# Planner constants of an fp32 attention and Fourier kernel on one core: durations, engine occupancy and latency apart

## The chip, the cores and the metric

The kernel runs on one core of one Trainium2 chip. The metric is the device time of one execution in microseconds (us). Before the change the median of three runs is 2807.93 us (2806.95 to 2810.59).

## The reference

Two independent blocks, whose results stand side by side in the output (2048 x 2048 fp32). Block A is attention with 32 heads of 32 columns that share one key and one value (multi-query). Block B is a Fourier mixing layer, the real part of a two-dimensional transform, written as products with four constant matrices.

```
q = (x @ wq) as 32 heads of 32;  k = x @ wk;  v = x @ wv      # x 2048x1024
p = softmax(q k^T / sqrt(32));   A = concat_heads(p @ v) @ wo
a = xB @ hid_re^T;  b = xB @ hid_im^T                          # 2048x1024
B = seq_re @ a - seq_im @ b                                    # seq: 2048x2048
out = concat([A, B], axis=-1)
```

## The kernel before

**Products.** Every large product other than attention's output is made of fp32r pieces. An operand is split into a high part (a cast to fp32r, tile names ending in h) and a low part (the operand minus its high part, ending in l); a block of 128 x 512 is summed over high times high, low times high and high times low. One group of `rest` has 12 to 48 such matmuls into one PSUM bank (psb). Right operands are tiles r, rh, rl, left ones m, mh, ml. The Fourier block's two stages are each done with seven products of half size (`PRODUCTS`), so operands are often sums of two blocks, which GpSimd adds. Some of these sums are stored once and loaded again (as). The high part is cast by VectorE (by ScalarE at the start of the kernel), the low part is subtracted by GpSimd, or by VectorE when the planner finds GpSimd late. Results leave PSUM through tile h and are added up in DRAM through tile y.

**Attention.** A unit is one of 32 pairs of a block of 512 queries and a group of four heads; it has 32 steps. A step has two parts. A *row* (`row`) is two matmuls into pss, 128 queries against 1024 keys; VectorE takes the row maximum (nm), ScalarE the exponentials and their sum. Only the maximum and the sum are kept. A *column* (`col`) is two matmuls into pst, the scores transposed with the maximum already subtracted inside the product; ScalarE takes the exponential into p. When the columns of four key chunks (eight steps) are there, `pv` multiplies them with v: a **burst** of matmuls with 32-column weights into a psb bank, the four heads at four places of the array. An fp32 matmul of a burst stands once in the program and as two records in the trace. `pv(k)` issues a burst whole; `pv(k, 0)` and `pv(k, 1)` issue its halves with a column and rows between. There are 128 bursts. pss has two buffers, pst one, psb two banks that groups of products, bursts and a small transpose (ident) share. After each unit VectorE turns the sums into factors, and the transpose brings the maxima into rows for the next pass.

**What sets the order.** Nothing is ordered at run time. The program is written by a planner in the same file. `Plan` keeps, for ScalarE, VectorE, GpSimd and the DMA queue of SP, the time from which the engine is free; `Plan.task` takes the engines that may do a task, its duration, what it depends on and a priority, and `Plan.run` (called up to the time `T` at which TensorE stands) starts the most urgent task that is known. A task that is finished makes its successors known, after the latency `LAG` of the engine that takes them. TensorE's stream is written by the main loop: at time `T` it puts the next burst, column, row or product of `rest` (the "fill") whose dependencies the plan holds to be done; each matmul costs `MM`, a burst `PV_US`, and a result is ready `MM_END` after the last one. Where nothing is ready, `T` moves on. So a planned duration decides on which instruction stands where, for all engines, and the order is fixed before the kernel runs. `prepare` makes the tasks of an operand (load, sum, high, low), `open_unit` those of a unit. A burst is cut in two where `STEP` times the steps that remain exceeds the matmul time that remains by more than `SPARE` allows:

```
if n + 2 * NB < total and STEP * (total - n) > (BODY - fill) * MM + (total - n) * (4 * MM + PV_US[4] / 8) - SPARE:
    pv(k, 0)
```

All engine instructions go through one helper and stand at its line, L57, in the profile; they are told apart by tile names.

Of the kernel before, what the change touches and what calls it, by code (L numbers as in the profile page):

```python
# [9 lines left out]
F32 = mybir.dt.float32  # L10
F32R = mybir.dt.float32r
# [27 lines left out]
ORDER_1, TURNED, ORDER_2 = (4, 1, 2, 3, 0, 6, 5), (3, 4, 5), (1, 0, 4, 2, 3, 5, 6)  # L39


MM, MM_END, PV_US, T_US = 0.232, 0.17, {2: 1.95, 4: 3.65}, 0.3
NB = 4
EXTRA = 2
LAG = {"act": 0.1, "dve": 0.1, "pool": 0.15, "sp": 0.3, "pe": 0.1}
ISSUE, RATE, FLIGHT = 0.42, 300.0, 2.0

# [17 lines left out]
class Plan:  # L65
# [50 lines left out]
    def run(self, until):  # L116
        while True:
            best = self.next()
            if best is None or best[0] > until:
                return  # L120
            at, e = best
            r, t = min((x for x in self.known[e] if x[0] <= at), key=lambda x: (x[1].prio, x[1].seq))
            for f, _ in t.engines:
                self.known[f] = [x for x in self.known[f] if x[1] is not t]
            t.on = e
            t.emit(e) if len(t.engines) > 1 else t.emit()
            us = t.us[e] if isinstance(t.us, dict) else t.us
            end = self.free[e] = at + us
            if e == "sp":
                self.dma = max(self.dma, end) + t.kb / RATE  # L130
                end = self.dma + FLIGHT
            self.finish(t, at, end)
# [48 lines left out]
def tile_kernel(ctx: ExitStack, tc, xT, wq, wkv, wo, xbT, wT, cT, out):  # L181
    nc = tc.nc
    te = Ordered(tc, nc.tensor)
    act = Ordered(tc, nc.scalar)
    dve = Ordered(tc, nc.vector)
    gp = Ordered(tc, nc.gpsimd)
    sp = Ordered(tc, nc.sync)
    eng = {"act": act, "dve": dve, "pool": gp}
    scale = float(DH) ** -0.5
    plan = Plan()  # L190
# [46 lines left out]
    ohr = Ring(misc, "oh", 1, [P, W], F32R)  # L237
    ovr = Ring(misc, "ov", 1, [P, W], F32)
    rbr = Ring(misc, "rb", 1, [P, W], F32)
# [278 lines left out]
    def prepare(it):  # L518
        kind, at = it.kind, it.need
        early = at < START  # L520
        hs, ls = (it.split[0], None) if it.split else (hir[kind].take(), lor[kind].take())
        hs.users.append(it.used)
        src = [landed[k] for k in it.after]
        if it.pre:
            def fetch(a):
                t = (hir if a == 0 else lor)[kind].make((hs, ls)[a])
                d = it.pre()[a]
                t = t[:, :d.shape[1]]
                move(t, d)
                if a:  # L530
                    it.lo = t
                else:
                    it.hi = t
            h = plan.task("sp", ISSUE, lambda: fetch(0), deps=[*hs.deps, *src], prio=at - 30, kb=256, order=o_hi[kind])
            l = plan.task("sp", ISSUE, lambda: fetch(1), deps=[*hs.deps, *src], prio=at - 30, kb=256, order=[h])
            o_hi[kind] = [l]
            it.ready = [h, l]
            return
        loads, it.t, it.raw = [], [None] * len(it.srcs), []
        for a, (ap, _) in enumerate(it.srcs):  # L540
            slot = it.room[0] if it.room else raw[kind][a].take()
            it.raw.append(slot)

            def load(a=a, ap=ap, slot=slot):
                d = ap()
                if it.room:
                    t = slot.tile[:, it.room[1]].bitcast(F32)
                else:
                    t = raw[kind][a].make(slot)
                if kind == "m":  # L550
                    t = t[:, :d.shape[1], :d.shape[2]]
                it.t[a] = t
                sp.dma_start(t.rearrange("p (a b) -> p a b", a=d.shape[1]) if kind == "r" and len(d.shape) == 3 else t, d)
            deps = slot.deps if not it.room else [before[it].ready[1]] if it in before else []
            o_load[kind] = [plan.task("sp", ISSUE, load, deps=[*deps, *src], prio=at - 30, kb=256, order=o_load[kind])]
            loads += o_load[kind]
        got = loads
        if len(it.srcs) > 1:
            def comb():
                (gp.tensor_add if it.srcs[1][1] > 0 else gp.tensor_sub)(it.t[0], it.t[0], it.t[1])  # L560
            got = [plan.task("pool", 1.33, comb, deps=loads, prio=at)]
            it.raw[1].users += got

        def high(on):
            if it.split and kind == "r":
                t = hs.tile
                it.hi, it.lo = (t[:, 2 * it.split[1] + x].bitcast(F32R) for x in range(2))
            elif it.split:
                t = hs.tile[:, it.split[1]]
                it.hi, it.lo = (t[:, x * 8 * DH:(x + 1) * 8 * DH].rearrange("p (a b) -> p a b", a=4).bitcast(F32R)  # L570
                                for x in range(2))
            else:
                it.hi, it.lo = hir[kind].make(hs), lor[kind].make(ls)
            if kind == "m" and not it.split:
                _, n, w = it.t[0].shape
                it.hi, it.lo = it.hi[:, :n, :w], it.lo[:, :n, :w]
            act.activation(it.hi, it.t[0], AF.Copy) if on == "act" else dve.tensor_copy(it.hi, it.t[0])
        h = plan.task((("act", 0.0), ("dve", 0.3)) if early else (("dve", 0.0), ("act", 1e6)), 0.65, high,
                      deps=[*got, *hs.deps], prio=at, order=[] if it.split else o_hi[kind])
        if not it.split:  # L580
            o_hi[kind] = [h]
        l = plan.task((("dve", 0.0), ("pool", 1.0)) if early else (("pool", 0.0), ("dve", 0.8 if kind == "r" else 2.5)), {"dve": 0.75, "pool": 1.33},
                      lambda on: eng[on].tensor_sub(it.lo, it.t[0], it.hi.bitcast(F32)), deps=[h], prio=at)
        it.raw[0].users.append(l)
        it.ready = [h, l]
# [22 lines left out]
    first_p = -1e5  # L608

    def open_unit(u):  # L610
        b, g = units[u]
        U = Unit()
# [11 lines left out]
        for r in range(SU):  # L624
            s = u * SU + r
            i, j = divmod(r, 2)

            def top(r=r, s=s, i=i, j=j):
                if r == 0:
                    nmr.make(U.nm), lsr.make(U.ls)  # L630
                dve.tensor_reduce(U.nm.tile[:, j, i:i + 1], rowps[s], axis=AX.X, op=ALU.max, negate=True)
            mx = plan.task("dve", 1.23, top, deps=[rowT[s], *(U.nm.deps if r == 0 else ())], prio=first_p + s - 44)
            plan.task("act", 1.14, lambda s=s, i=i, j=j: act.activation(
                rowps[s], rowps[s], AF.Exp, bias=U.nm.tile[:, j, i:i + 1], accum_out=U.ls.tile[:, j, i:i + 1]),
                deps=[mx], prio=first_p + s - 43.6, into=rexp[s],
                order=[cexp[s - SU - LEAD - EXTRA]] if s >= SU + LEAD + EXTRA else [])

# [48 lines left out]
        for c in range(NC):  # L686
            slot = pr.take()
            slot.users.append(pvH[u][c // 2])
            for hp in range(2):
                n = u * SU + 2 * c + hp  # L690

                def ex(n=n, hp=hp, slot=slot, c=c):
                    if hp == 0:
                        pt[u, c] = pr.make(slot)
                    act.activation(pt[u, c][:, 2 * hp:2 * hp + 2], colps[n], AF.Exp)
                plan.task("act", 1.05, ex, deps=[colT[n], *(slot.deps if hp == 0 else ())], prio=first_p + n, into=cexp[n])

        U.ov = ovr.take()
        U.add = []
# [5 lines left out]
                    dve.tensor_add(U.ov.tile, U.ov.tile, pvps[u, k])  # L705
            U.add.append(plan.task("dve", 0.7, ad, deps=[pvT[u][k], *(U.ov.deps if k == 0 else U.add[-1:])], prio=-1e3))
        U.oh = ohr.take()
        a = plan.task("dve", 0.76, lambda: dve.tensor_mul(U.ov.tile, U.ov.tile, U.rb.tile), deps=[U.add[-1], *U.inv], prio=-5)
        U.rb.users.append(a)
        h = plan.task("dve", 0.45, lambda: dve.tensor_copy(ohr.make(U.oh), U.ov.tile), deps=[a, *U.oh.deps], prio=-5)  # L710
        if u + 1 < NU:
            l = plan.task("dve", 0.75, lambda: dve.tensor_sub(U.ov.tile.bitcast(F32R), U.ov.tile, U.oh.tile.bitcast(F32)),
                          deps=[h], prio=-5)
            U.oh.users.append(l)
            U.oh.users.append(store(lambda: oh_d[b][g], lambda: U.oh.tile, [h], level(u * SU + 48), key=("oh", b, g), bits=True))
            U.ov.users.append(store(lambda: ol_d[b][g], lambda: U.ov.tile, [l], level(u * SU + 48), key=("ol", b, g), bits=True))
        else:
            s = rbr.take()
            l = plan.task("dve", 0.75, lambda: dve.tensor_sub(rbr.make(s, F32R), U.ov.tile, U.oh.tile.bitcast(F32)),
                          deps=[h, *s.deps], prio=-5)  # L720
            U.low = s
        U.end = [h, l]
# [127 lines left out]
        issue(o.us, emit, [o.done])  # L850
        bank_task[b] = o.freed

    SLACK, AHEAD, RUN, STEP, SPARE = 0.05, 30, 20, 2.55, 10.0

    def odd_ones():
        for o in odds:
# [51 lines left out]
    s = k = 0  # L908
# [146 lines left out]
```

## Time and profile before

| | |
|---|---|
| runs, median (lowest to highest) | 2807.93 us (2806.95 to 2810.59) |
| the profiled execution's own time | 2807.72 us |
| its span, first to last instruction | 2805.9 us |
| granted TensorE clock, mean | 0.998 |
| DMA | 518.64 MB, 185 GB/s over the span |
| TensorE: products, rows, columns, bursts | 5664, 2048, 2048, 4096 records |
| ScalarE: row and column exponentials | 1024 of 1086 ns, 1024 of 1027 ns |
| VectorE: row maxima | 1024 of 1221 ns |

The busy time of an engine is a union over the span; an instruction of ScalarE or VectorE may start before the record of the one ahead has ended, so durations add up to more than the engine's busy time. A matmul's record is longer than the distance to the next one, since they are pipelined; the time of TensorE's stream is read from start to start.

### The profile page before, as it was taken

To read this page: it belongs to the slowest core of one execution; us is meant where nothing else is said; L and a number is where in the kernel's file an instruction comes from. 1 tells how busy PE (TensorE), PEld (TensorE's weight loads), DVE (VectorE), ACT (ScalarE), POOL (GpSimd) and SP (SyncE) were. 2 spreads that over 40 slices of the span, in tenths; PEclk is the share of its full clock that TensorE was granted. 3 is DMA by queue.
4 is the path that set the end of the run, shared out by engine and by line. 5 is a ranking of instruction groups with operands and counts; after the bars stand their busy time and mean duration, and the time that the engine had idled before them with its cause. 6 is when DMAs were issued, how large, how long until landed. Compare 5 with 4: busy or idle time off the path is not lost.

```text
span 2805.9 us, 40813 instructions
## 1 busy us (share of the span) xinstructions
PE 2783.4 (99%) x13904; PEld 1929.3 (69%) x13904; DVE 1972.9 (70%) x2394; ACT 2225.0 (79%) x3204; POOL 1418.1 (51%) x1073
## 2 busy tenths in 40 slices
PE   8999999999999999999999999999999999999999
PEld 6876666666666666666676676776666776767667
DVE  6887767768878777778667668678777787676510
ACT  5688888888888888898888887888787888878741
POOL 2664425547666446535526537568768566540000
PEclk9999999999999999999999999999999999999999
DMA  9664546657776547635736726458749654453445
GB/s 291 189 195 136 168 142 201 216 188 248 234 239 204 163 148 244 210 110 165 253 95 203 231 89 200 148 173 263 248 156 290 189 168 153 132 154 114 143 147 158
DMA packets 336465, 518.64 MB, mean 185 GB/s; under 512 B 35712, under 2 KB 100736, under 8 KB 336256
## 3 DMA queue, kind: packets, MB, share of 16 engines
q1 hardware_dynamic: 336256, 516.04, 58.6%
q8 instruction: 109, 1.79, 0.3%
q14 instruction: 100, 0.82, 0.1%
HBM read 376.70 MB, written 138.15 MB: 183 GB/s over the span
## 4 chain that ended last, share of the span: by engine, by line
PE 93%; DVE 4%; DMA 1%; POOL 1%; issue 1%; ACT 0%; SPq 0%; POOLq 0%; DVEq 0%; ACTq 0%
PE psb L57 59%; PE pst L57 17%; PE pss L57 17%; DVE nm L57 1%; DVE rh L57 1%; DMA r<-as 1%; DVE h L57 0%; ACT pss L57 0%; POOL ml L57 0%; DVE mh L57 0%; POOL rl L57 0%; DVE md L57 0%; DMA a<-y 0%; DMA y<-a 0%; DVE l L57 0%
## 5 line engine op out<-in xcount | busy, mean ns | idle before, releaser
L57 DVE TENSOR_REDUCE nm<-pss 128x1 f32<-128x1024 f32 x1024 | 1238.4, 1221 | 427.6 <-PE pss L57 424.7
L57 ACT ACTIVATE p<-pst 128x1024 f32<-128x1024 f32 x1024 | 1051.4, 1027 | 350.6 <-PE pst L57 347.8
L57 ACT ACTIVATE pss<-pss,nm 128x1024 f32<-128x1024 f32 x1024 | 1111.6, 1086 | 131.1 <-DVE nm L57 129.0
L57 PE MATMUL psb<-rh,mh 128*128 128x512 f32 x1756 | 694.0, 395 | 2.1 <-DVE h L57 1.6
L57 PE MATMUL psb<-rh,ml 128*128 128x512 f32 x1756 | 690.7, 393 | 0.0
L57 PE MATMUL psb<-rl,mh 128*128 128x512 f32 x1756 | 690.6, 393 | 0.0
L57 PE MATMUL pst<-qst,kst 128*128 128x512 f32 x2048 | 663.1, 405 | 0.1
L57 POOL TENSOR_TENSOR ml<-m,mh 128x512 fp32r<-128x512 f32 x330 | 436.8, 1324 | 416.8 <-DVE mh L57 285.9
L57 PE MATMUL pss<-kst,qst 128*128 128x512 f32 x2048 | 624.9, 396 | 4.8 <-ACT pss L57 4.7
L57 PEld LDWEIGHTS pst<-qst,kst 128*128 128x128 f32 x2048 | 369.9, 188 | 230.3 <-issue 110.7
L57 PE MATMUL psb<-p,v 128*32 128x512 f32 x4096 | 478.4, 597 | 0.5 <-DVE h L57 0.5
L57 PEld LDWEIGHTS pss<-kst,qst 128*128 128x128 f32 x2048 | 382.2, 188 | 101.4 <-ACT pss L57 12.6
L57 POOL TENSOR_TENSOR m<-m,m 128x512 f32<-128x512 f32 x200 | 264.1, 1321 | 246.2 <-DMA m<-in_cT_dram 159.4
L57 PEld LDWEIGHTS psb<-rh,mh 128*128 128x128 f32 x1756 | 329.6, 188 | 82.5 <-DVE h L57 4.2
L57 PEld LDWEIGHTS psb<-rl,mh 128*128 128x128 f32 x1756 | 330.0, 188 | 77.4
L57 PEld LDWEIGHTS psb<-rh,ml 128*128 128x128 f32 x1756 | 329.6, 188 | 77.3
L57 POOL TENSOR_TENSOR y<-y,h 128x512 f32<-128x512 f32 x192 | 258.6, 1352 | 227.6 <-DVE h L57 200.3
L57 POOL TENSOR_TENSOR rl<-r,rh 128x512 fp32r<-128x512 f32 x190 | 253.3, 1339 | 228.0 <-DVE rh L57 214.5
L57 PEld LDWEIGHTS psb<-p,v 128*32 128x32 f32 x4096 | 113.8, 109 | 262.6 <-issue 253.3
L57 DVE CAST mh<-m 128x512 fp32r<-128x512 f32 x329 | 198.7, 606 | 13.8 <-PE psb L57 12.2
L57 ACT ACTIVATION_READ_ACCUMULATOR pss<-pss,nm 128x1 f32 x1024 | 207.5, 203 | 0.0
L57 POOL TENSOR_TENSOR r<-r,r 128x512 f32<-128x512 f32 x120 | 158.0, 1320 | 60.5 <-DMA r<-a 32.0
(77 smaller groups left out, 981.9 us busy)
## 6 DMA issues: line engine op xcount, KB each, us to landing
m<-in_cT_dram SPq DMA_DIRECT2D x384, 256.0 KB, 3.7
r<-a SPq DMA_DIRECT2D x192, 256.0 KB, 4.2
y<-a SPq DMA_DIRECT2D x128, 256.0 KB, 3.4
a<-y SPq DMA_DIRECT2D x128, 256.0 KB, 2.8
r<-in_wT_dram SPq DMA_DIRECT2D x96, 256.0 KB, 4.1
m<-in_xbT_dram SPq DMA_DIRECT2D x96, 256.0 KB, 3.3
y<-y SPq DMA_DIRECT2D x96, 256.0 KB, 3.9
as<-r SPq DMA_DIRECT2D x80, 256.0 KB, 4.4
```

The source lines that it names most:

```text
L57: return lambda *a, **k: self.tc.keep_in_program_order(f(*a, **k))
```

## The change

The planner's constants change, and two lines of its account. The time until an engine is free again is now less than a task's duration by `OVER` (0.1 us on ScalarE, 0.08 on VectorE, 0.06 on GpSimd), so that occupancy and latency are apart; durations of tasks are set anew; a matmul's result counts as ready 0.1 us after its time, not 0.17; `STEP` is 2.45, not 2.55. `T_US` was not used. Nothing else differs: the same tasks, tiles and buffers.

```diff
-MM, MM_END, PV_US, T_US = 0.232, 0.17, {2: 1.95, 4: 3.65}, 0.3
+MM, MM_END, PV_US = 0.232, 0.1, {2: 1.98, 4: 3.65}
+OVER = {"act": 0.1, "dve": 0.08, "pool": 0.06, "sp": 0.0}
...
-            end = self.free[e] = at + us
+            end = at + us
+            self.free[e] = max(end - OVER[e], at + us / 2)
...
-        h = plan.task((("act", 0.0), ("dve", 0.3)) if early else (("dve", 0.0), ("act", 1e6)), 0.65, high,
+        h = plan.task((("act", 0.0), ("dve", 0.3)) if early else (("dve", 0.0), ("act", 1e6)), 0.72 if kind == "r" else 0.62, high,
...
-            mx = plan.task("dve", 1.23, top, deps=[rowT[s], *(U.nm.deps if r == 0 else ())], prio=first_p + s - 44)
-            plan.task("act", 1.14, lambda s=s, i=i, j=j: act.activation(
+            mx = plan.task("dve", 1.22, top, deps=[rowT[s], *(U.nm.deps if r == 0 else ())], prio=first_p + s - 44)
+            plan.task("act", 1.22, lambda s=s, i=i, j=j: act.activation(
...
-                plan.task("act", 1.05, ex, deps=[colT[n], *(slot.deps if hp == 0 else ())], prio=first_p + n, into=cexp[n])
+                plan.task("act", 1.055, ex, deps=[colT[n], *(slot.deps if hp == 0 else ())], prio=first_p + n, into=cexp[n])
...
-    SLACK, AHEAD, RUN, STEP, SPARE = 0.05, 30, 20, 2.55, 10.0
+    SLACK, AHEAD, RUN, STEP, SPARE = 0.05, 30, 20, 2.45, 10.0
```

The other lines of the diff set durations of smaller tasks of VectorE and GpSimd: the low parts (0.75 to 0.8, 1.33 to 1.34), and the end of a unit (0.76 to 0.77, 0.45 to 0.6, 0.75 to 0.8).

What this does to the order is seen at three places of TensorE's stream. The first is a burst about a quarter into the program. In a row, pst is a column, pss a row, psb from rh or rl a product, psb from p and v a burst; a whole burst has 16 instructions. Before:

```order
L57 MATMUL psb<-p,v 32x512 x8
L57 MATMUL pst<-qst,kst 128x512 x2
L57 MATMUL pss<-kst,qst 128x512 x4
L57 MATMUL psb<-p,v 32x512 x8
L57 MATMUL pst<-qst,kst 128x512 x2
L57 MATMUL psb<-rh,mh 128x512
L57 MATMUL pss<-kst,qst 128x512 x2
```

The same stretch after the change, with the step ahead of the burst:

```order
L58 MATMUL pst<-qst,kst 128x512 x2
L58 MATMUL psb<-rl,mh 128x512
L58 MATMUL psb<-rh,ml 128x512
L58 MATMUL psb<-rh,mh 128x512
L58 MATMUL pss<-kst,qst 128x512 x2
L58 MATMUL psb<-rl,mh 128x512
L58 MATMUL psb<-rh,ml 128x512
L58 MATMUL pst<-qst,kst 128x512 x2
L58 MATMUL psb<-p,v 32x512 x16
L58 MATMUL pst<-qst,kst 128x512 x2
L58 MATMUL pss<-kst,qst 128x512 x4
```

The burst is whole, with one column and two rows behind it, and the step ahead of it, from one column to the next, has nine matmuls. In the whole program 188 bursts and halves became 135.

The second place is the transpose (ident) that ends a unit, before, where it falls between two groups of products: the product behind it is the first of a group, and uses the bank that the product ahead of it ended.

```order
L57 MATMUL psb<-rl,mh 128x512
L57 MATMUL psb<-rh,ml 128x512
L57 MATMUL psb<-ident,m_1_270 128x128
L57 MATMUL pss<-kst,qst 128x512 x2
L57 MATMUL psb<-rh,mh 128x512
```

After, the transpose of the same unit stands behind a whole burst and the rows that follow it:

```order
L58 MATMUL psb<-p,v 32x512 x16
L58 MATMUL pst<-qst,kst 128x512 x2
L58 MATMUL pss<-kst,qst 128x512 x4
L58 MATMUL psb<-ident,m_1_270 128x128
L58 MATMUL psb<-rh,mh 128x512
```

There the burst has taken its own bank, and the distance from a group's end to the next use of its bank has grown.

The third place is the end of the last unit, where the products of `rest` run out; the pss rows behind the last burst belong to the last eight groups. Before:

```order
L57 MATMUL pst<-qst,kst 128x512 x2
L57 MATMUL psb<-rh,ml 128x512
L57 MATMUL psb<-rh,mh 128x512
L57 MATMUL psb<-rl,mh 128x512
L57 MATMUL psb<-rh,ml 128x512
L57 MATMUL psb<-rh,mh 128x512
L57 MATMUL psb<-rl,mh 128x512
L57 MATMUL psb<-rh,ml 128x512
L57 MATMUL psb<-rh,mh 128x512
L57 MATMUL psb<-rl,mh 128x512
L57 MATMUL psb<-rh,ml 128x512
L57 MATMUL psb<-rh,mh 128x512
```

Two products (psb from rl and rh) and the last burst follow these rows. After:

```order
L58 MATMUL pst<-qst,kst 128x512 x2
L58 MATMUL psb<-rh,mh 128x512
L58 MATMUL psb<-rl,mh 128x512
L58 MATMUL psb<-rh,ml 128x512
L58 MATMUL pst<-qst,kst 128x512 x4
L58 MATMUL psb<-p,v 32x512 x16
L58 MATMUL pss<-rh,mh 128x512
```

The products ended earlier against the columns, and the last two columns and the last burst follow each other with none between.

More of the change, by code (lines that the diff above doesn't have):

```diff
@@ L581, in prepare @@
             o_hi[kind] = [h]
-        l = plan.task((("dve", 0.0), ("pool", 1.0)) if early else (("pool", 0.0), ("dve", 0.8 if kind == "r" else 2.5)), {"dve": 0.75, "pool": 1.33},
+        l = plan.task((("dve", 0.0), ("pool", 1.0)) if early else (("pool", 0.0), ("dve", 0.8 if kind == "r" else 2.5)), {"dve": 0.8, "pool": 1.34},
                       lambda on: eng[on].tensor_sub(it.lo, it.t[0], it.hi.bitcast(F32)), deps=[h], prio=at)
@@ L707, in open_unit @@
         U.oh = ohr.take()
-        a = plan.task("dve", 0.76, lambda: dve.tensor_mul(U.ov.tile, U.ov.tile, U.rb.tile), deps=[U.add[-1], *U.inv], prio=-5)
+        a = plan.task("dve", 0.77, lambda: dve.tensor_mul(U.ov.tile, U.ov.tile, U.rb.tile), deps=[U.add[-1], *U.inv], prio=-5)
         U.rb.users.append(a)
-        h = plan.task("dve", 0.45, lambda: dve.tensor_copy(ohr.make(U.oh), U.ov.tile), deps=[a, *U.oh.deps], prio=-5)
+        h = plan.task("dve", 0.6, lambda: dve.tensor_copy(ohr.make(U.oh), U.ov.tile), deps=[a, *U.oh.deps], prio=-5)
         if u + 1 < NU:
-            l = plan.task("dve", 0.75, lambda: dve.tensor_sub(U.ov.tile.bitcast(F32R), U.ov.tile, U.oh.tile.bitcast(F32)),
+            l = plan.task("dve", 0.8, lambda: dve.tensor_sub(U.ov.tile.bitcast(F32R), U.ov.tile, U.oh.tile.bitcast(F32)),
                           deps=[h], prio=-5)
@@ L718, in open_unit @@
             s = rbr.take()
-            l = plan.task("dve", 0.75, lambda: dve.tensor_sub(rbr.make(s, F32R), U.ov.tile, U.oh.tile.bitcast(F32)),
+            l = plan.task("dve", 0.8, lambda: dve.tensor_sub(rbr.make(s, F32R), U.ov.tile, U.oh.tile.bitcast(F32)),
                           deps=[h, *s.deps], prio=-5)
```

## The prediction

> **What bounds the kernel now.** I read the page's first and fourth parts first.
>
> ```profile
> span 2805.9 us, 40813 instructions
> PE 2783.4 (99%) x13904; PEld 1929.3 (69%) x13904; DVE 1972.9 (70%) x2394; ACT 2225.0 (79%) x3204; POOL 1418.1 (51%) x1073
> PE 93%; DVE 4%; DMA 1%; POOL 1%; issue 1%; ACT 0%; SPq 0%; POOLq 0%; DVEq 0%; ACTq 0%
> ```
>
> TensorE is busy nearly all the time and 93% of the chain that ends last, so the time is the length of TensorE's own stream plus the moments at which it waits. Nothing done elsewhere saves anything unless it shortens one of these two. The profiled execution took 2807.72 us, 1.8 more than its span, and 0.2 under the median of the three runs.
>
> Next, the timeline of TensorE at a burst of output matmuls (psb<-p,v; 16 records are a half, 32 a whole).
>
> ```profile
> 1301.97 1.09 PE L57 MATMUL pss<-kst,qst 128*128 128x512 f32 x4
> 1302.99 1.92 PE L57 MATMUL psb<-p,v 128*32 128x512 f32 x16
> 1304.85 0.73 PE L57 MATMUL pst<-qst,kst 128*128 128x512 f32 x2
> 1305.41 0.40 PE L57 MATMUL psb<-rh,mh 128*128 128x512 f32 x1
> ...
> 1317.93 0.63 PE L57 MATMUL pst<-qst,kst 128*128 128x512 f32 x2
> ...
> 1358.32 0.63 PE L57 MATMUL pst<-qst,kst 128*128 128x512 f32 x2
> 1358.88 3.64 PE L57 MATMUL psb<-p,v 128*32 128x512 f32 x32
> 1362.45 0.74 PE L57 MATMUL pst<-qst,kst 128*128 128x512 f32 x2
> 1363.03 1.10 PE L57 MATMUL pss<-kst,qst 128*128 128x512 f32 x4
> ```
>
> From 1305.41 to 1317.93 lie 54 matmuls without a burst: 12.52 / 54 = 0.232 us from start to start, one **step** below. A half burst: from 1301.97 to 1305.41 are 3.44 us with six other matmuls in them, 3.44 - 6 x 0.232 = 2.05. A whole burst: from 1358.32 to 1363.03 are 4.71 us with four others, 4.71 - 4 x 0.232 = 3.78. These prices hold the slower change into and out of a burst. Two halves cost 4.10, **0.32 us more than one whole**.
>
> Third, what TensorE waited for.
>
> ```profile
> PE psb L57 <- ACT p L57: 5.6, 1, 5.6
> PE pss L57 <- ACT pss L57: 4.7, 5, 1.9
> PE psb L57 <- DVE m L57: 3.8, 3, 3.2
> PE psb L57 <- DVE h L57: 2.1, 7, 0.5
> PE psb L57 <- POOL ml L57: 1.8, 1, 1.8
> ```
>
> The first and the last are the start of the kernel, before and at its first products (7.4 together). There remain about 10.6 us in the body: even a perfect order can take no more from waits than this and what follows them.
>
> **The change, part by part.**
>
> *Bursts.* By the order of TensorE's instructions, before has 68 whole bursts and 120 halves, after 121 whole and 14 halves: 53 pairs become whole. 53 x 0.32 = **-17.0 us**, all on TensorE's stream. Everything else that TensorE issues keeps its count. What the halves hid was ScalarE: the softmax's exponentials stand still during a burst. I cost that under the cadence below.
>
> *Banks.* At nine places in the order before, all while halves are used, a group of products starts too soon after the last use of its bank: a group ends, a transpose (ident) follows into the other bank, one pair of score matmuls, then the next group.
>
> ```profile
> 699.91 0.39 PE L57 MATMUL psb<-rh,ml 128*128 128x512 f32 x1
> 700.17 0.71 PE L57 MATMUL pss<-kst,qst 128*128 128x512 f32 x2
> 700.41 0.69 DVE L57 TENSOR_SCALAR h<-psb 128x512 f32<-128x512 f32 x1 [0.24 <-PE psb L57]
> 701.16 0.50 PE L57 MATMUL psb<-rh,mh 128*128 128x512 f32 x1 [0.28 <-DVE h L57]
> ```
>
> The bank is free 701.16 - 699.91 = 1.25 us after its last matmul; without the wait the next product would have started at 700.17 + 2 x 0.232 = 700.63, so 0.53 at most was lost here, 0.28 by the row's own idle time. Between the sum of the idle (2.1) and 9 x 0.53 = 4.8 I take 3.5. In the order after, the transpose stands inside a group, and one place with a distance under 1.25 us is left (4 steps, 0.9 us): **-3.2 us**.
>
> *The end.* Before, 13 products stand between the last pair of column scores (pst) and the last burst. After, the products run out: three of them, then two pairs of pst at once, then the burst. A pst pair can follow the last one only when its exponential is done.
>
> ```profile
> 1338.08 0.63 PE L57 MATMUL pst<-qst,kst 128*128 128x512 f32 x2
> 1338.75 1.02 ACT L57 ACTIVATE p<-pst 128x1024 f32<-128x1024 f32 x1 [0.20 <-PE pst L57]
> 1344.78 1.09 ACT L57 ACTIVATE pss<-pss,nm 128x1024 f32<-128x1024 f32 x1 [0.76 <-DVE nm L57]
> 1346.79 1.09 ACT L57 ACTIVATE pss<-pss,nm 128x1024 f32<-128x1024 f32 x1
> ```
>
> That is 0.67 from the start of the pair to its exponential, 1.02 for it, and 0.04 to release TensorE (the 0.04 is a row below): 1.74 us. The order gives 5 steps (1.16), then 2 (0.46), then 2 again before the burst: 0.58 + 1.28 + 1.28 = **+3.1 us**. There is no cover: no products are left. Each of these stops is under 1.3 us; that matters for the clock, next.
>
> *The planner's numbers.* ScalarE's and VectorE's instructions are now planned to follow each other sooner (about 0.1 us less occupancy), and the order follows. Before, successive pst pairs stand nine steps apart 461 times and ten 258 times, mostly in turn; now nine 703 times and ten 16 times. Nine steps are 2.09 us. ScalarE can do this: two successive row exponentials, with the column one between, start 1346.79 - 1344.78 = 2.01 apart when nothing holds them. So it is hidden, with 0.08 us to spare in each step. The chain through VectorE has this form (from the chain of waits):
>
> ```profile
> 2111.91 1.14 DVE nm L57
> ...
> 2113.14 1.21 ACT pss L57 x2
> 2114.35 0.04 issue
> 2114.40 0.73 PE pss L57 x2
> 2115.13 1.15 PE psb L57 x3
> 2116.28 0.85 PE pss L57 x2
> 2117.13 0.85 PE psb L57 x2
> 2117.99 0.79 PE pst L57 x2
> 2118.78 0.23 PE psb L57
> ```
>
> A row of scores needs the maximum and the exponential of the row but one before: 0.67 + (2114.40 - 2111.91) = 3.16 us. At nine steps each, rows but one stand 18 steps, 4.18 us apart: slack 1.02. At nine and ten in turn it was 4.41: slack 1.25. What eats slack is a VectorE cast:
>
> ```profile
> L57 DVE CAST mh<-m 128x512 fp32r<-128x512 f32 x329 | 198.7, 606 | 13.8 <-PE psb L57 12.2 <-POOL rl L57 1.0 <-POOL m L57 0.4
> L57 DVE CAST rh<-r 128x512 fp32r<-128x512 f32 x216 | 151.6, 713 | 12.6 <-DMA r<-as 8.4 <-POOL r L57 2.6 <-DMA r<-in_wo_dram 0.8
> 1345.64 1.29 POOL L57 TENSOR_TENSOR r<-r,r 128x512 f32<-128x512 f32 x1 [2.09 <-DMA as<-r]
> 1345.73 1.49 DVE L57 CAST mh<-m 128x512 fp32r<-128x512 f32 x1
> 702.35 0.46 DVE L57 CAST mh<-m 128x512 fp32r<-128x512 f32 x1
> ```
>
> One takes 0.46 alone and 1.49 when it starts just behind a GpSimd instruction; by the means, (606 - 460) / 1030 and (713 - 460) / 1030, 14 to 25% are long. The planner now counts 0.62 and 0.72, near the means, so a long one is 1.03 late against a short one. One alone stays inside the slack either way; two in a row cost 2.06 - 1.02 = 1.04 now, 0.81 before, 1.3 times as much. The waits for ACT pss (4.7) grow by about a third, 1.5, and with the moved waits for DVE m I take **+2 us**. Its ends: all 10.6 - 2.1 = 8.5 us of these waits gone, with what follows them, about -12; or doubled, +12. What follows them: from 2114.40 to 2118.78 eleven matmuls took 4.38 us where eleven steps are 2.55, so a stop of 1.9 us cost another 1.8 behind it.
>
> The Trainium skill ("TensorE: Matmul & The Clock Gate", part 1) has it that the clock halves after an idle window of about 3.4 us. The trace differs: the slow steps follow a stop of 1.9 us already. By the page none of the stops at the new order's end would be followed by slow steps; by the rows, which show none under 1.9 us, one may be, for 1.8 us more.
>
> Fourteen subtractions move from GpSimd to VectorE, two single instructions from ScalarE to it; at VectorE's 70% they are hidden, and cost at most their own 0.7 us each, 11 us, were VectorE the bound. SP issues the same transfers, in an order that follows the plan; the DMA terms of the planner are not changed, so a late landing can stop TensorE as before, elsewhere.
>
> *Sum.* -17.0 - 3.2 + 3.1 + 2 = -15.1. 2805.9 - 15.1 = 2790.8 of span, 2792.6 as a run, 2792.8 beside the median.
>
> **The rivals.**
>
> *The stops go too.* Better durations give an order in which nothing in the body waits: -12 in place of +2, so 2779. For it: nine bank waits are gone by the order itself. Against: the other stops come from long casts and late landings, which a planner with one number each cannot see.
>
> *The spare time was needed, in part.* Doubled stops, +12 in place of +2, and one more clock drop: 2805. For it: the slack falls from 1.25 to 1.02 and to 0.08 per step on ScalarE. Against: ScalarE is 79% busy and whole bursts ran in the second half of before.
>
> *Slower: long casts in pairs.* The Trainium skill ("SBUF — State Buffer", on the shared port pair) says that VectorE's fast copies and GpSimd exclude each other for a whole instruction. The 1.49 us row agrees. As a mechanism of this kernel: GpSimd is 51% busy, so half of the casts could be long, not a quarter. Each pair in a nine-step stretch costs 1.04 us. To lose the 15 us that I forecast takes 15 pairs among 121 whole bursts, one in eight; to be over 0.2% slower, 2813.5, takes 20 in all; one in four, 30 pairs, gives 2793 + 31 = 2824. Before, with 0.81 each, only 4.7 us of such waits stood in the whole run, about six pairs. That makes it unlikely.
>
> *It doesn't do what it says.* The counts of bursts stand in the order; only the price of a whole one in the first half of the run, where before has halves alone, isn't shown. At 4.10 for it (no gain) the time would be 2810.
>
> **How the numbers follow.** 0.2% is 5.6 us, about what a measurement of this kernel can tell from no change: faster is under 2802.3, slower over 2813.5. Forecast (2785 to 2800) 0.63; stops gone (2777 to 2785) 0.15; spare time needed (2800 to 2811) 0.17, a third of it still under 2802.3; slower 0.04; no gain from bursts 0.01. Faster: 0.63 + 0.15 + 0.06 = 0.84; same 0.12; slower 0.04. The range leaves out the low end of the second case and the upper half of the third: 2780 to 2805. I predict 2793.
>
> **What would show it.** In the profile after, 121 bursts of 32 records and 14 of 16, each whole one 3.78 us by the same count, in the first half of the run too. TensorE's waits for DVE h near zero; three stops of 0.6 to 1.3 us just before the last burst. The waits for ACT pss at 6 rather than 4.7 us; over 12 would bear out the second or third rival, and then with long casts ahead of the late maximum in the chain. I am wrong if the bursts are as said and the time is not near 2793: then the stops are what I mis-sized.

## The result, and the profile after

| | before | after |
|---|---|---|
| median of six runs | 2808.5 us | 2826.4 us (2823.3 to 2828.8) |
| ratio to before | | 1.0063, 95% interval 1.005 to 1.0076 |
| profiled execution: its own time, span | 2807.72, 2805.9 us | 2828.76, 2827.0 us |

The change made the kernel 18 us slower, where 15 us less were forecast. The page of the kernel after, its span, busy times and shares of the chain that ended last:

```profile
span 2827.0 us, 40786 instructions
PE 2777.7 (98%) x13904; PEld 1933.9 (68%) x13904; DVE 1997.3 (71%) x2410; ACT 2200.0 (78%) x3202; POOL 1405.6 (50%) x1059
PE 86%; DVE 8%; DMA 2%; ACT 1%; issue 1%; POOL 1%; SPq 0%; ACTq 0%; DVEq 0%; POOLq 0%
```

TensorE's share of that chain fell from 93 to 86%, and VectorE's doubled from 4 to 8%. The timeline of TensorE at a burst in the first half of the program, where before had halves alone:

```profile
180.22 0.63 PE L58 MATMUL pst<-qst,kst 128*128 128x512 f32 x2
180.78 3.64 PE L58 MATMUL psb<-p,v 128*32 128x512 f32 x32
184.35 0.74 PE L58 MATMUL pst<-qst,kst 128*128 128x512 f32 x2
184.93 1.10 PE L58 MATMUL pss<-kst,qst 128*128 128x512 f32 x4
```

Its price is 184.93 - 180.22 - 4 x 0.232 = 3.78 us, as forecast. So the stream got shorter as it should. What TensorE waited for (total, times, longest):

```profile
PE pss L58 <- ACT pss L58: 23.4, 21, 4.6
PE psb L58 <- DVE m L58: 8.6, 7, 2.2
PE psb L58 <- ACT p L58: 4.8, 1, 4.8
PE psb L58 <- DVE ov L58: 2.4, 4, 1.2
PE pst L58 <- ACT p L58: 1.8, 3, 1.2
PE psb L58 <- DVE h L58: 1.7, 1, 1.7
```

The waits for a row's exponential went from 5 of 4.7 us in all to 21 of 23.4, those for the end of a unit (DVE m) from 3.8 to 8.6. A budget makes kernels comparable below. The **stream** is all of TensorE's instructions at the prediction's prices (a step for each of 9760 matmuls, 2259.4 in all, which is 0.2315 us each; 3.784 a whole burst, 2.05 a half, 3.8 for the transposes). The **stops** are the rest: the time less the stream and less 11.6 us, the same for every kernel (in the trace of before 5.6 before the first matmul, 4.2 from the last one's start to the end, 1.8 outside the span). They hold the waits and also the slower steps around them.

| | stream | stops | time |
|---|---|---|---|
| before | 2766.5 | 30.4 | 2808.5 |
| after | 2749.8 | 65.0 | 2826.4 |

The stream lost 16.7 us and the stops gained 34.6. (The expectations below say 67 stops for after; that is its profiled execution, which took 2828.76 us.) TensorE's waits after its first matmul sum to 12.9 us in the trace of before and to 40.2 in that of after, so most of the new stops are waits; slower steps behind them take most of the rest.

Where they come from is seen at 440.10 us, in the timeline of the kernel after. TensorE first (in brackets the idle time ahead and what ended it):

```profile
429.92 3.64 PE L58 MATMUL psb<-p,v 128*32 128x512 f32 x32
434.06 1.08 PE L58 MATMUL pss<-kst,qst 128*128 128x512 f32 x4
...
437.31 0.40 PE L58 MATMUL psb<-rh,ml 128*128 128x512 f32 x1
440.10 0.73 PE L58 MATMUL pss<-kst,qst 128*128 128x512 f32 x2 [2.39 <-ACT pss L58]
440.67 0.40 PE L58 MATMUL psb<-rh,mh 128*128 128x512 f32 x1
440.90 0.40 PE L58 MATMUL psb<-rl,mh 128*128 128x512 f32 x1
```

VectorE in the same stretch, where a cast from r to rh or from m to mh makes a high part:

```profile
430.03 0.69 DVE L58 COPY h<-psb 128x512 f32<-128x512 f32 x1 [1.55 <-PE psb L58]
430.64 1.50 DVE L58 CAST mh<-m 128x512 fp32r<-128x512 f32 x1
432.06 3.26 DVE L58 CAST rh<-r 128x512 fp32r<-128x512 f32 x3
435.24 1.78 DVE L58 TENSOR_TENSOR rl<-r,rh 128x512 fp32r<-128x512 f32 x1
436.94 0.68 DVE L58 COPY ov<-psb 128x512 f32<-128x512 f32 x1
437.54 2.34 DVE L58 TENSOR_REDUCE nm<-pss 128x1 f32<-128x1024 f32 x2
```

And GpSimd:

```profile
430.57 1.28 POOL L58 TENSOR_TENSOR m<-m,m 128x512 f32<-128x512 f32 x1
431.80 1.46 POOL L58 TENSOR_TENSOR y<-y,h 128x512 f32<-128x512 f32 x1
433.23 1.47 POOL L58 TENSOR_TENSOR ml<-m,mh 128x512 fp32r<-128x512 f32 x1
435.06 3.10 POOL L58 TENSOR_TENSOR rl<-r,rh 128x512 fp32r<-128x512 f32 x2 [0.36 <-DVE rh L58]
```

The planner puts four casts and a subtraction on VectorE while TensorE is in a burst and no rows come. Planned at 0.62 (m), 0.72 (r) and 0.8, each 0.08 less for the engine, they take 0.54 + 3 x 0.64 + 0.72 = 3.2 us. They took 6.3 (430.64 to 436.94): in these rows a cast that starts while a GpSimd instruction runs ends behind it, again and again. The two rows at 434.06 stand in line behind them; the first maximum starts at 437.54 and TensorE stops for 2.39 us. A late maximum delays the exponential, and that the next row but one. Ahead of each of the 21 waits for a row in this trace, within 11 us, stands at least one instruction of VectorE on operands in SBUF that took more than 0.9 us.

### The profile page after: what moved, and what is told of

It reads as the page before. It is cut to its first block, busy times and chain, and to the rows that moved or that the text cites. A ratio compares the mean times of both kernels' runs of the same rounds, so it can differ in the third digit from the quotient of the medians.

```text
span 2827.0 us, 40786 instructions
## 1 busy us (share of the span) xinstructions
PE 2777.7 (98%) x13904; PEld 1933.9 (68%) x13904; DVE 1997.3 (71%) x2410; ACT 2200.0 (78%) x3202; POOL 1405.6 (50%) x1059
## 4 chain that ended last, share of the span: by engine, by line
PE 86%; DVE 8%; DMA 2%; ACT 1%; issue 1%; POOL 1%; SPq 0%; ACTq 0%; DVEq 0%; POOLq 0%
PE psb L58 54%; PE pss L58 16%; PE pst L58 16%; DVE nm L58 3%; DVE rh L58 1%; ACT pss L58 1%; DVE ov L58 1%; DMA r<-as 1%; DVE rl L58 1%; DVE mh L58 1%; DVE md L58 1%; DVE h L58 0%; DMA m<-in_wq_dram 0%; DVE m L58 0%; DMA r<-in_xT_dram 0%
## 5 line engine op out<-in xcount | busy, mean ns | idle before, releaser
L58 PE MATMUL pss<-kst,qst 128*128 128x512 f32 x2048 | 628.6, 397 | 23.7 <-ACT pss L58 23.4
L58 PE MATMUL psb<-p,v 128*32 128x512 f32 x4096 | 467.4, 595 | 1.7 <-DVE h L58 1.7
L58 POOL TENSOR_TENSOR rl<-r,rh 128x512 fp32r<-128x512 f32 x181 | 245.7, 1364 | 233.1 <-DVE rh L58 212.8
L58 DVE TENSOR_TENSOR ov<-ov,psb 128x512 f32<-128x512 f32 x96 | 65.2, 679 | 191.5 <-PE psb L58 191.5
L58 DVE CAST mh<-m 128x512 fp32r<-128x512 f32 x330 | 187.6, 569 | 11.2 <-PE psb L58 9.6
```

What stands on the lines that cost most here:

```text
L58: return lambda *a, **k: self.tc.keep_in_program_order(f(*a, **k))
```

## The experiments

Theory 1: VectorE's instructions on operands in SBUF, held up by GpSimd, make the stops; the new order leaves less room for them. Theory 2: ScalarE has no reserve when columns stand nine steps apart (the cadence of nine), whatever VectorE does. Theory 3, formed on the way: the planner's order is one of many that its rules could have drawn, and that of before is a favourable draw.

### The same order, with a cast that GpSimd can't hold up

```diff
-            act.activation(it.hi, it.t[0], AF.Copy) if on == "act" else dve.tensor_copy(it.hi, it.t[0])
+            act.activation(it.hi, it.t[0], AF.Copy) if on == "act" else dve.tensor_reduce(
+                it.hi, it.t[0].unsqueeze(len(it.t[0].shape)), axis=AX.X, op=ALU.max)
```

A maximum over one element is the element itself, written out as fp32r. The planner isn't told, so every engine keeps its order. On after:

> The kernel after, same order on every engine, but VectorE's cast of an operand's high part is written as a maximum over one element, which should take its 512 elements one by one without being held up by GpSimd (some 0.6 us each time, in place of 0.42 or 1.1 to 1.5). Theory 1 (VectorE instructions held up by GpSimd, stacked ahead of row maxima, make TensorE's stops): the stops fall from 67 us to 35 or less, time 2785 to 2800. Theory 2 (the cadence of nine leaves ScalarE no reserve, whatever VectorE does): the stops stay, 2820 or more.

On before:

> The kernel before with the same replacement of the cast. Theory 1: the stops of the body (about 14 of 30 us that aren't the start or the bank waits) halve, time 2798 to 2804. Theory 2: 2808, as before.

Measured: 2800.9 us on after's order (ratio to before 0.9968, 0.9958 to 0.9977) and 2800.4 on before's (0.9972, 0.9961 to 0.9984). By the medians the cast gives 25.5 us in one order and 8 in the other, and 39.5 and 22.3 us of stops are left. On before that is what theory 1 expected. On after it is far from theory 2's 2820, but theory 1 had asked for 35 us of stops or less, and the time is just above its range: the casts are most of the cause there and not all of it. The groups of casts in the kernel after (count, busy time, mean in ns, idle time ahead and what ended it):

```profile
L58 DVE CAST mh<-m 128x512 fp32r<-128x512 f32 x330 | 187.6, 569 | 11.2 <-PE psb L58 9.6 <-issue 1.1 <-DMA m<-in_cT_dram 0.2
L58 DVE CAST rh<-r 128x512 fp32r<-128x512 f32 x216 | 157.9, 744 | 15.5 <-DMA r<-as 11.0 <-POOL r L58 1.9 <-DMA r<-a 1.9
```

The same groups in a_cast1:

```profile
L58 DVE TENSOR_REDUCE mh<-m 128x512 fp32r<-128x512 f32 x330 | 223.4, 677 | 12.0 <-PE psb L58 11.0 <-issue 0.3 <-DMA m<-in_cT_dram 0.2
L58 DVE TENSOR_REDUCE rh<-r 128x512 fp32r<-128x512 f32 x216 | 143.1, 676 | 18.2 <-DMA r<-as 13.4 <-POOL r L58 3.3 <-DMA r<-a 1.3
```

In sum the casts, counted by their records, take longer, 330 x 0.677 + 216 x 0.676 = 369 us in place of 330 x 0.569 + 216 x 0.744 = 348. VectorE does not get less work; it gets the same every time: the casts take 0.35 to 2.1 us in the trace of after, the maxima 0.62 to 0.69 here. At the place of the stop at 440.10 us the same work took 4.0 us instead of 6.3, and the row came without a wait:

```profile
427.89 0.68 DVE L58 TENSOR_REDUCE mh<-m 128x512 fp32r<-128x512 f32 x1
428.48 1.86 DVE L58 TENSOR_REDUCE rh<-r 128x512 fp32r<-128x512 f32 x3
430.26 1.67 DVE L58 TENSOR_TENSOR rl<-r,rh 128x512 fp32r<-128x512 f32 x1
435.02 0.73 PE L58 MATMUL pss<-kst,qst 128*128 128x512 f32 x2
```

TensorE's waits in a_cast1:

```profile
PE psb L58 <- DVE m L58: 8.6, 7, 3.1
PE pss L58 <- ACT pss L58: 6.4, 7, 1.9
PE psb L58 <- ACT p L58: 4.8, 1, 4.8
```

The waits for rows fall from 23.4 to 6.4 us; those for DVE m stay. They hang on other instructions, which the next pair takes in.

### The same order, with VectorE's casts and arithmetic in SBUF out of GpSimd's way

The same maximum over one element, as a helper, in place of VectorE's casts and subtractions, of its small instructions between units and of those at the end of a unit, for example:

```diff
+    def one(to, of):
+        dve.tensor_reduce(to, of.unsqueeze(len(of.shape)), axis=AX.X, op=ALU.max)
...
-        a = dv(0.35, lambda: dve.tensor_sub(U.md.tile[:, 0], T["m"], U.nm.tile[:, 0]), a)
+        a = dv(0.35, lambda: one(U.md.tile[:, 0], T["m"]), a)
```

> The order of after, with every VectorE instruction whose operands lie in SBUF written as a maximum over one element of one operand, so that none shares anything with GpSimd. It leaves out VectorE's part of the subtractions and the arithmetic at the end of a unit, so the output isn't the reference's; what waits for what stays. If GpSimd's hold-up of VectorE explains the rest: stops 15 to 22 (start, end and small ones), time 2776 to 2785. If late transfers or the cadence make them: 30 or more, 2792 to 2801.

> The same on the order of before, with the same parts left out. Hold-up: stops 15 to 20, time 2793 to 2799, so that the order of after is faster by about the 15 us that its stream is shorter. Otherwise: 2800, as with the cast alone.

Measured: 2782.8 us on after's order (ratio 0.9908, 0.9889 to 0.9928) and 2790.2 on before's (0.9932, 0.9917 to 0.9948). Stops: 21.4 and 12.1, as theory 1 expected on after and even fewer than it expected on before. So in after's order 43.6 of the 65 us go with the hold-up, in before's 18.3 of 30.4: 25.3 of the 34.6 us of new stops. The hold-up goes both ways, and the pairs take out both: GpSimd's instructions on two tiles took 1.32 to 1.36 us on average, group by group, in after, and 1.29 in a_nolock. The waits of TensorE in b_nolock:

```profile
PE psb L57 <- ACT p L57: 5.0, 1, 5.0
PE psb L57 <- DVE h L57: 1.6, 6, 0.3
PE psb L57 <- DVE m L57: 1.3, 1, 1.3
PE psb L57 <- DVE p L57: 0.7, 1, 0.7
```

A small instruction between units, its group in the kernel after, once with its mean and once with its shortest, median and longest:

```profile
L58 DVE TENSOR_TENSOR md<-mm,nm 128x16 f32<-128x16 f32 x64 | 26.9, 450 | 0.7
L58 DVE TENSOR_TENSOR md<-mm,nm x64: 158/175/1275, 139.5 to 2669.0; 128x16 f32<-128x16 f32 x64
```

And in a_nolock:

```profile
L58 DVE TENSOR_REDUCE md<-mm 128x16 f32<-128x16 f32 x64 | 8.5, 163 | 0.7
```

Not one wait for a row is left in b_nolock. Even an instruction of 16 elements a partition takes 450 ns on average and up to 1275, and 163 without GpSimd in its way; several of them stand in a chain ahead of the transpose, which is the wait for DVE m. Here at last the order of after is faster than that of before, by 7.4 us in the medians of four runs each (every run of after's order is below every one of before's, though the two intervals overlap), not by the 16.7 of its stream: 9 us of stops are left that the hold-up doesn't explain. The profiled execution of a_nolock took 2789.43 us, the longest of its four, so its waits are more than the median has. Those for rows are:

```profile
PE pss L58 <- ACT pss L58: 8.2, 5, 3.1
```

And VectorE's waits for loads of stored sums there, more than for any other transfer:

```profile
DVE rh L58 <- DMA r<-as: 20.8, 11, 4.1
```

The longest of them ends the wait ahead of a cast, and the row maxima stand behind it:

```profile
2134.42 0.69 DVE L58 TENSOR_REDUCE rh<-r 128x512 fp32r<-128x512 f32 x1 [4.15 <-DMA r<-as]
2135.03 2.35 DVE L58 TENSOR_REDUCE nm<-pss 128x1 f32<-128x1024 f32 x2
2137.59 1.22 PE L58 MATMUL pss<-kst,qst 128*128 128x512 f32 x2 [3.12 <-ACT pss L58]
```

VectorE waited 20.8 us for such loads, and a wait for one of about 3 us or more lies in the 11 us ahead of each of the five stops. That the loads cause these stops is read from this one execution; no run took them away.

### The draw

Three orders by the rules of before, with one number off that should not matter, and two by those of after:

```diff
-    SLACK, AHEAD, RUN, STEP, SPARE = 0.05, 30, 20, 2.55, 10.0
+    SLACK, AHEAD, RUN, STEP, SPARE = 0.05, 30, 20, 2.45, 10.0
```

> The kernel before with STEP at 2.45 alone: 67 whole bursts and 122 halves, nine and ten steps in turn as in before; stream 2766.8 us. A control: if STEP made the change, 2795 or less; if what matters are the other constants, and another order of the same kind has about the same stops, 2803 to 2815.

```diff
-ISSUE, RATE, FLIGHT = 0.42, 300.0, 2.0
+ISSUE, RATE, FLIGHT = 0.42, 301.0, 2.0
```

> The kernel before with the planner's transfer rate at 301 in place of 300: a change of 0.3% in a number that has nothing to do with the question, so that the order is drawn anew by the same rules (65 whole bursts, 126 halves; stream 2767.4 us, 1 more than before). If the order of before is a favourable draw (theory 3): 2813 to 2825, as the run with STEP alone. If its constants make it fast: 2805 to 2812.

> The same with 299: 68 whole bursts and 120 halves, the stream of before to 0.1 us. Theory 3: 2813 to 2825. Constants: 2805 to 2812.

> The kernel after with the transfer rate at 301: 115 whole bursts, 26 halves; stream 2751.6 us, 2 more than after. Theory 3 (the draw): anywhere in 2808 to 2832. If the new constants make about 67 us of stops whatever the draw: 2826 to 2834.

> The kernel after with 299: 117 whole bursts, 22 halves; stream 2751 us. Theory 3: anywhere in 2808 to 2832. Constants: 2826 to 2834.

| | ratio to before | stops, us | time, us |
|---|---|---|---|
| before | 1 | 30.4 | 2808.5 |
| b_draw2 (299) | 1.0006 (0.9996 to 1.0015) | 30.9 | 2809.0 |
| b_draw1 (301) | 1.0016 (1.0007 to 1.0026) | 35.0 | 2814.0 |
| b_step | 1.0046 (1.0028 to 1.0063) | 43.8 | 2822.2 |
| a_draw1 (301) | 1.0034 (1.0018 to 1.005) | 54.2 | 2817.4 |
| a_draw2 (299) | 1.0051 (1.0036 to 1.0066) | 60.3 | 2822.9 |
| after | 1.0063 (1.005 to 1.0076) | 65.0 | 2826.4 |

STEP alone changes hardly any burst (67 whole, not 68) and still costs 13.7 us, above both ranges that were expected: an order that is the same by its counts differs by up to that much. Of the two other draws of before, 301 came out as theory 3 expected and 299 as its rival did; those of after lie in the wide range of theory 3, below the rival's. So theory 3 is right in part: before is the best of four draws of its rules (b_step counted with them), after the worst of three of its own. But the two groups don't overlap in stops: their means are 35 and 60. So of the 34.6 us of new stops some 25 go with the rules, and some 10 with the draw. In time the groups do overlap, 2808.5 to 2822.2 and 2817.4 to 2826.4; the rules of after lose 9 us on the mean of these few orders, half of what the one pair showed. This split by rules and draw is another one than that by hold-up and the rest, though the numbers are alike.

### Which of the planner's numbers

One part undone in after, or done alone in before; STEP at its old value in after; and after planned with the held-up durations:

```diff
-OVER = {"act": 0.1, "dve": 0.08, "pool": 0.06, "sp": 0.0}
+OVER = {"act": 0.0, "dve": 0.08, "pool": 0.06, "sp": 0.0}
```

> The kernel after, planned without the shorter occupancy of ScalarE (0.1 to 0): the order has 46 whole bursts and 164 halves, and columns nine and ten steps apart in turn, as before; stream 2773.5 us by the prices of a step and a burst (after: 2750). Theory 2: the stops fall to about 30, time 2815. Theory 1: VectorE is still planned with its short occupancy, stops 45 to 60, time 2830 to 2845.

```diff
-OVER = {"act": 0.1, "dve": 0.08, "pool": 0.06, "sp": 0.0}
+OVER = {"act": 0.1, "dve": 0.0, "pool": 0.06, "sp": 0.0}
```

> The kernel after, planned without the shorter occupancy of VectorE (0.08 to 0): 114 whole bursts and 28 halves, columns nine steps apart; stream 2752 us. Theory 1: the stops fall to 45 or less, time 2808 or less. Theory 2: they stay near 67, time 2828 to 2834.

```diff
+OVER = {"act": 0.1, "dve": 0.0, "pool": 0.0, "sp": 0.0}
...
-            end = self.free[e] = at + us
+            end = at + us
+            self.free[e] = max(end - OVER[e], at + us / 2)
```

> The kernel before with ScalarE's numbers of after alone (occupancy 0.1 less, 1.22 and 1.055 us): 77 whole bursts, 102 halves, columns nine steps apart; stream 2763.7 us. If the cadence of nine takes the reserve that a held-up VectorE needs: stops 50 or more, 2825 or more. If VectorE's numbers do it: about 35, 2807 to 2815.

b_dve is the same with 0.0 for act and 0.08 for dve, and ScalarE's durations as in before.

> The kernel before with VectorE's occupancy of after alone (0.08 less): 70 whole bursts, 116 halves, nine and ten steps in turn; stream 2765.9 us. Cadence: stops about 35, 2807 to 2815. VectorE's numbers: 50 or more, 2825 or more.

```diff
-    SLACK, AHEAD, RUN, STEP, SPARE = 0.05, 30, 20, 2.45, 10.0
+    SLACK, AHEAD, RUN, STEP, SPARE = 0.05, 30, 20, 2.55, 10.0
```

> The kernel after with STEP back at 2.55: 78 whole bursts and 100 halves, columns nine steps apart as in after; stream 2763.3 us. If VectorE's work that piles up during a whole burst is what stops TensorE, fewer whole bursts give fewer stops, about 50: 2825. If the cadence of nine alone does it, stops stay 67: 2842.

```diff
-        h = plan.task((("act", 0.0), ("dve", 0.3)) if early else (("dve", 0.0), ("act", 1e6)), 0.72 if kind == "r" else 0.62, high,
+        h = plan.task((("act", 0.0), ("dve", 0.3)) if early else (("dve", 0.0), ("act", 1e6)), 1.1 if kind == "r" else 1.0, high,
...
-        l = plan.task((("dve", 0.0), ("pool", 1.0)) if early else (("pool", 0.0), ("dve", 0.8 if kind == "r" else 2.5)), {"dve": 0.8, "pool": 1.34},
+        l = plan.task((("dve", 0.0), ("pool", 1.0)) if early else (("pool", 0.0), ("dve", 0.8 if kind == "r" else 2.5)), {"dve": 1.7, "pool": 1.34},
```

> The kernel after, with the same instructions and the same shorter occupancies, but planned with what VectorE's instructions on operands in SBUF take when GpSimd holds them up: casts 1.1 and 1.0 us (0.72 and 0.62 in after), subtractions 1.7, the end of a unit 1.1 to 1.3, the small ones between units 0.8. 112 whole bursts, 32 halves, nine steps; stream 2752.6 us. If the stops come from planning means where the instruction is short or long (theory 1): stops 40 or less, time 2795 to 2806. If any tight order stops as much, because of late transfers or ScalarE (rival): stops 55 to 70, time 2820 or more.

| | VectorE's occupancy | stream | stops | time (interval of the ratio to before) |
|---|---|---|---|---|
| a_act0 | short | 2773.5 | 51.1 | 2836.2 (1.0084 to 1.0114) |
| b_dve | short | 2765.9 | 45.7 | 2823.2 (1.0037 to 1.0067) |
| a_step | short | 2763.3 | 52.4 | 2827.3 (1.0051 to 1.0082) |
| a_dve0 | full | 2752.0 | 50.7 | 2814.3 (1.001 to 1.0029) |
| b_act | full | 2763.7 | 37.8 | 2813.1 (1.0005 to 1.0023) |
| a_res | short, longer durations | 2752.6 | 45.1 | 2809.3 (0.9997 to 1.0016) |

Theory 2 falls, by the pairs above most of all: they keep the cadence of nine, and the stops go from 65 to 39.5 and 21.4. Here too, ScalarE's old numbers leave 51 us of stops in after, not 30, and its new ones alone (b_act, columns nine steps apart) have 38, inside the range of before's draws.

Which number of the planner makes the stops, these runs don't tell. Without ScalarE's shorter occupancy after loses 14 us of stops, without VectorE's 14 as well (a_dve0 came out between the two expectations). Done alone in before, VectorE's adds 15 and ScalarE's 7, so they lean towards VectorE's (b_dve lies just under what was expected for that). Each of these is one draw, whose spread is about as large, so it is an indication and not proof. The casts' new durations, the earlier end of a matmul's result and GpSimd's occupancy were not undone alone.

a_step came out near its first expectation: fewer whole bursts took 12.6 of the stops, and the stream paid 13.5 for it. a_res, which counts with the held-up durations, removes 20 us of stops for 3 of stream, less than theory 1 expected (45 remain, not 40) and more than its rival; it comes back to the time of before, but not under it. What is left in its trace are many small waits, 17 of 10.2 us in all for rows, the longest 1.5.

### Toward a faster kernel

c3 and c4 plan the one-by-one cast (the maximum over one element) at its own 0.68 us and leave the low parts to GpSimd after the start; c4 also has VectorE's full occupancy. a_dve0_cast1 is the order of a_dve0 with that cast.

```diff
-        l = plan.task((("dve", 0.0), ("pool", 1.0)) if early else (("pool", 0.0), ("dve", 0.8 if kind == "r" else 2.5)), {"dve": 0.8, "pool": 1.34},
+        l = plan.task((("dve", 0.0), ("pool", 1.0)) if early else (("pool", 0.0), ("dve", 1e6)), {"dve": 1.3, "pool": 1.34},
```

> Both together: the one-by-one cast, planned at its 0.68 us, the subtraction of low parts left to GpSimd alone after the start, the end of a unit and the small instructions planned as in a_res. 111 whole bursts, 34 halves; stream 2752.9 us. Theory 1: stops 30 or less, time 2794 or less, faster than before and after. Rival: 2805 or more.

> The order of a_dve0 (after without VectorE's shorter occupancy, 2814 us) with the one-by-one cast. The cast gave 25 us on the order of after and 8 on that of before, where stops were 67 and 30; here they are 50, so about 17: 2794 to 2800, the fastest complete kernel of this study. If the gains don't add up: 2801 or more.

> A newly drawn order: VectorE's full duration as occupancy, the one-by-one cast planned at 0.68, the low parts' subtraction on GpSimd alone after the start, somewhat longer durations for the end of a unit and the small instructions. 112 whole bursts, 32 halves; stream 2752.6 us. With stops as in c3 (38): 2802. If full occupancy helps as it did in after: stops 25 to 30, 2789 to 2795.

Measured: c3 2802.7 (0.9971 to 0.999), a_dve0_cast1 2801.2 (0.9965 to 0.9986), c4 2804.5 (0.9974 to 0.9993), with 38.2, 37.6 and 40.3 us of stops. All three are faster than before and after, none faster than the cast alone on either order (2800.4 and 2800.9). The gains don't add up: the cast on a_dve0's order gave 13 us, not 17, c3 missed its 2794 by 9, and c4 its 2795 by 10 and its other expectation, 2802, by 3. What a version under 2795 needs is not settled.

## Why the prediction was wrong

*Bursts: right.* 121 whole and 14 halves, 3.78 us each also in the first half, and the stream 16.7 us shorter.

*Banks: the places are gone, the saving isn't there.* Seven waits for DVE h became one, of another kind (1.7 us, a burst waiting for a bank). But four waits for DVE ov, which empties a burst's bank, came up (2.4 us, 0.2 before), so the waits put down to a bank went from 2.3 to 4.1 us, where 3.2 less were forecast. Out of GpSimd's way they are 1.6 in before's order and 1.7 in after's.

*The end: too high.* Two of the three stops stand there; the third does not. The timeline of TensorE in the kernel after:

```profile
2771.51 0.62 PE L58 MATMUL pst<-qst,kst 128*128 128x512 f32 x2
2773.25 0.74 PE L58 MATMUL pst<-qst,kst 128*128 128x512 f32 x2 [0.42 <-ACT p L58]
2775.16 0.73 PE L58 MATMUL pst<-qst,kst 128*128 128x512 f32 x2 [1.17 <-ACT p L58]
2775.82 3.64 PE L58 MATMUL psb<-p,v 128*32 128x512 f32 x32
```

From start to start, less the steps between, the two cost 0.58 and 1.45 us. The burst starts 0.66 us behind its last columns and shows no idle time: its first matmuls take earlier key chunks, and the last chunk's turn comes some 2.7 us later, when the exponential is done. 2.0 us, not 3.1.

*The planner's numbers: the step that failed.* "The waits for ACT pss (4.7) grow by about a third, 1.5, and with the moved waits for DVE m I take +2 us. Its ends: ... about -12; or doubled, +12." Measured: ACT pss +18.7, DVE m +4.8, all stops +34.6. The term of +2 us was mis-sized, and its upper end of +12 too. The mechanism was named: the rival "slower: long casts in pairs" gave 1.04 us a pair and 20 pairs for a loss that can be measured, and the profile has 21 waits of 23.4 / 21 = 1.1 us. That the means agree is partly luck: the single waits go from 0.2 to 4.6 us, and not all stand behind a pair of casts. By the rival's own sum 21 pairs give 2815, not 2826; the waits for DVE m and the slow steps are not in it. What was wrong is the number of the waits, 21 where some six were reckoned before, and with it the chance of 0.04.

The step scaled the count in one trace by the ratio of two slacks. That count belonged to a favourable order, as the draws show: the waits for ACT pss are 4.7 us in before, 6.1, 8.8 and 15.7 in the other three orders of its kind, and 15.5 to 23.4 in those of after. And the slack was worked out between two bursts for two casts, while at the largest stops, as at 440.10 us, the work piles up inside a burst: three or four casts and a subtraction in a row. The share of long casts was read well and did not change: 108 of 545 took over 1 us in before, 103 of 546 in after. So it is not that more casts were held up; by the trace, they now stand where rows wait behind them. Nor did the step count the small instructions of a unit's end as things that GpSimd holds up.

*The hold-up.* The Trainium skill ("SBUF — State Buffer", section "Who interferes with whom") says that VectorE's fast copies and GpSimd exclude each other for a whole instruction. The pairs on one order agree, 43.6 us in the order of after. The prediction quoted it for casts and left out the two-operand instructions, small ones among them, for which the Trainium skill states the same where both operands are in SBUF and GpSimd's instruction reads SBUF.

*The slow steps: not as read.* The prediction took a stop of 1.9 us as enough for slow steps, and none under that. In the trace of before the stop of 1.78 us at the start (the wait for POOL ml) is followed by steps of 0.43 us, which the prediction overlooked. The rows at 440.10 above have a stop of 2.39 us with products 0.23 us apart behind it. Length alone does not decide it. Behind stops in the body there are four such slow stretches in the trace of after (waits of 2.22, 1.92, 4.61 and 3.14 us) and two in that of before.

## What to carry to other kernels

Be wary of planning an order ahead with the mean of an instruction that has two modes: here, making VectorE's cast steady (2800.9 us) was worth more than planning it at its held-up duration (2809.3, one order). When a static order is already one of many drawn, compare a change of the planner with several draws of both rules: the count of rare stops in one trace says little about the next. And where the busiest engine gains on paper, price the reserve of the engine that feeds it at the point where work piles up, not on the average.

## What the runs showed of the hardware

A maximum over one element writes 128 x 512 fp32 elements as fp32r in 676 to 677 ns on average in each group of a_cast1, and in 690 at most. The cast that it replaces takes 0.42 us at the median in the kernel after and up to 2.1 where GpSimd is in its way. A subtraction of 128 x 16 elements takes 158 ns at its shortest and 450 on average there; the maximum in its place takes 163 on average, and 172 at most. Two products may follow each other at full pace behind a stop of 2.39 us and at 0.43 us behind one of 1.85.
